# Decayed block attention and a squared-ReLU feed-forward: the attention's results are placed 64 bytes off the other operands within 256 bytes of on-chip memory

## The chip, the core and the metric

The kernel runs as one program on one core of a Trainium2 chip. The metric is the device time of one execution in microseconds. Of the kernel before there are three timed runs, 636.74, 637.0 and 637.23 us, with a median of 637.0 us. Besides, one execution was profiled; it took 637.8 us, of which 636.1 us lie between its first and its last instruction (the span).

## What is computed

```python
# attention with a decay, per batch b and head h; block of 64 positions, S = 768, D = 64, 4 batches, 8 heads
for each block:
    intra = (qb @ kb.T * Dmask) @ vb               # Dmask[i, j] = lam ** (i - j) for i >= j, else 0
    inter = (qb * lam_pow) @ kv_state
    out   = intra + inter
    kv_state = lam ** 64 * kv_state + (kb * rev_pow).T @ vb
# feed-forward on x = out, seen as 3072 tokens x 512 features
h = maximum(x @ w_in, 0)                           # w_in 512 x 2048
y = (h * h) @ w_out                                # w_out 2048 x 512
```

## The kernel before

**The tokens and the tiles.** The 3072 tokens are 24 chunks of 128 positions of one batch (`CHUNKS`), and three chunks make one tile of `N` = 384 tokens, so there are eight tiles (`TILES`). For each chunk two attention units (`q` = 0 and 1, four heads each) produce the attention's result, transposed, so that features lie on the 128 partitions and tokens along them. The first eight chunks run through `unit_plain` in float32, the other sixteen through `unit_split`, where every operand of a product is split into a high and a low float32r part.

**The tiles `xh` and `xl`.** The result of a unit is written to the tile `x` of its token tile, also as a high part (a copy on ScalarE, lines 382 and 497) and a low part (a subtraction on VectorE, lines 383 and 498). `x` has two buffers; each has an `xh` and an `xl` of 4 x 384 words a partition. These are the "attention's results" of the title.

**The feed-forward (`ffn`).** For each token tile and each of 16 blocks `f` of the 2048 hidden features, `mm1` (line 515) multiplies 12 times: for `(wih, xh)`, `(wih, xl)` and `(wil, xh)` four products each, one for each quarter `cc` of the 512 features. The stationary operand is a 128 x 128 piece of the weights, loaded into TensorE by a weight load (LDWEIGHTS) ahead of each product, and the moving operand is 384 words a partition of `xh` or `xl`. That is 8 x 16 x 12 = 1536 products. ReLU and square follow on ScalarE and VectorE (lines 529 to 536) and give `gh` and `gl`. The second products (`mm2`, lines 521, 522 and 524) take 128 x 128 pieces of `gh` or `gl` as the stationary operand and the 512 words of `woh` or `wol` as the moving one: 9 for each `f`, 1152 in all. From the third token tile on, the second products of two `f` run in one go after the first products of both.

**The order of the work.** `Plan` holds each operation with a guessed duration, a key and its buffers; `order` simulates the five engines and writes one fixed order for each of them. That order does not depend on addresses. The early part of the program (`early=True`: the preparation of the weights from 64-bit words, and `unit_plain`) uses its own buffers `pnt`, `diag0`, `diag1`, `st` and `m` (`EARLY`); when all of it has been issued, `late()` gives that memory back and makes the buffers of `unit_split` (`LATE`) in the same place. A late buffer waits for the last use of the early buffers that it overlaps. The packets `pkt` are the first of them to be filled, by DMAs on the SP queue (line 408).

**Where the buffers lie.** Tiles of a pool lie one after the other in the order of the calls that make them. Each takes a whole number of 256-byte units of a partition, but for two small tables that `unit_plain` and `unit_split` use as scales: `wdec` (8 words, 32 bytes) and `lc` (4 words, in a place of 32 bytes). They are the last of the permanent tiles (`const`). So in the kernel before every permanent tile (`gh`, `gl`, `g`, `hold`, `s1`, `vd`, `xh`, `xl`, `rdec`, all weights) starts 128 bytes past a multiple of 512; the early buffers behind the tables start 64 bytes further, at 192 past a multiple of 256 (`pnt0` at 190144); and `late()` puts a tile `space` of 112 words (448 bytes) ahead of the late buffers, which takes them to 128 past a multiple of 512 again (`pkt0` at 190592). `xh0` lies at 31872 and `wih0` at 59008.

Of the kernel before, what the change touches and what calls it, by code (L numbers as in the profile page):

```python
# [9 lines left out]
F32 = mybir.dt.float32  # L10
# [7 lines left out]
B, H, S, D = 4, 8, 768, 64  # L18
DM, DFF = 512, 2048
P = 128  # L20
C = 128
NC_ = S // C
NP = H // 2
# [130 lines left out]
LATE = ("pkt", "ab", "ka", "vv", "pp", "z", "zl", "ss0", "ss1")  # L154
# [13 lines left out]
def kernel(ctx: ExitStack, tc: tile.TileContext, pn, pk, lamx, w, out):  # L168
    nc = tc.nc
    const = ctx.enter_context(tc.tile_pool(name="const", bufs=1))  # L170
# [17 lines left out]
    def make(pool, kinds):  # L188
        for k in kinds:
            tiles[k] = [pool.tile(*shapes[k], name=f"{k}{'_' if k[-1].isdigit() else ''}{i}") for i in range(SLOTS[k])]  # L190

    make(ps, ("bank", "h"))
    make(const, [k for k in SLOTS if k not in EARLY + LATE + ("bank", "h", "x")])
    tiles["x"] = [[const.tile([P, NCC, N], F32R, name=f"{n}{i}") for n in ("xh", "xl")] for i in range(SLOTS["x"])]
    rdec = const.tile([P, NP, C], F32, name="rdec")

    flip, zero = tiles["g"][-1][:, 0:P], tiles["ob"][-1]
# [3 lines left out]
    wil = [const.tile([P, NCC, P], F32R, name=f"wil{f}") for f in range(NF)]  # L201
    woh = [const.tile([P, DM], F32R, name=f"woh{f}") for f in range(NF)]
    wol = [const.tile([P, DM], F32R, name=f"wol{f}") for f in range(NF)]

    wdec = const.tile([P, H], F32, name="wdec")
    lc = const.tile([P, NP], F32, name="lc")
    make(phase.enter_context(tc.tile_pool(name="early", bufs=1)), EARLY)

    def late():
        phase.close()  # L210
        pool = ctx.enter_context(tc.tile_pool(name="late", bufs=1, reuse_waits="tile"))
        pool.tile([P, 112], F32, name="space")
        make(pool, LATE)

        for k in ("ss0", "ss1"):
            for s in tiles[k]:
                nc.gpsimd.memset(s.bitcast(F32), 0.0)
# [395 lines left out]
    with tc.manual_schedule():  # L613
        for o in done:
            if o.early is False and not opened:
                assert n_early == 0, "an earlier buffer is still in use"
                late()
                opened = True
            o.fn()
            n_early -= o.early is True  # L620
# [43 lines left out]
```

## Time and profile before

| | |
|---|---|
| timed runs | 636.74, 637.0, 637.23 us; median 637.0 us |
| profiled execution | 637.8 us, span 636.1 us |
| TensorE clock granted over the span | 0.999 |
| first products (line 515) | 1536, each 128 x 128 stationary, 384 words moving |
| second products (lines 521, 522, 524) | 1152, each 128 x 128 stationary, 512 words moving |
| moved by DMA | 57.24 MB, a mean of 90 GB/s |

In the rows of the profile PE is TensorE's products, PEld its weight loads, DVE VectorE, ACT ScalarE, POOL GpSimd and SP the engine that issues the DMAs. [...] A row of the timeline that ends in x4 merges four products of one line; the distance between the starts of two such rows is the time of four.

### The profile page before, as it was taken

To read this page: it belongs to the slowest core of one execution; us is meant where nothing else is said; L and a number is where in the kernel's file an instruction comes from. 1 tells how busy PE (TensorE), PEld (TensorE's weight loads), DVE (VectorE), ACT (ScalarE), POOL (GpSimd) and SP (SyncE) were. 2 spreads that over 40 slices of the span, in tenths; PEclk is the share of its full clock that TensorE was granted. 3 is DMA by queue.
4 is the path that set the end of the run, shared out by engine and by line. 5 is a ranking of instruction groups with operands and counts; after the bars stand their busy time and mean duration, and the time that the engine had idled before them with its cause. 6 is when DMAs were issued, how large, how long until landed. Compare 5 with 4: busy or idle time off the path is not lost.

```text
span 636.1 us, 9584 instructions
## 1 busy us (share of the span) xinstructions
PE 627.1 (99%) x3608; PEld 570.4 (90%) x3608; DVE 476.6 (75%) x1078; ACT 360.9 (57%) x841; POOL 5.7 (1%) x15
## 2 busy tenths in 40 slices
PE   9899999999999999999999999999999999999997
PEld 7689999888999999999999999999999999999996
DVE  5999999946876998588965999659994799633222
ACT  5887777656755665366743766445753657522221
POOL 2000000000000000000000000000000000000000
PEclk9999999999999999999999999999999999999999
DMA  8825555513311220231203312121310411000001
GB/s 290 272 102 169 193 168 172 226 53 134 113 51 50 100 65 35 84 116 49 100 1 99 100 56 94 50 100 50 100 51 0 149 50 51 1 30 22 0 1 49
DMA packets 15166, 57.24 MB, mean 90 GB/s; under 512 B 1808, under 2 KB 1808, under 8 KB 15120
## 3 DMA queue, kind: packets, MB, share of 16 engines
q1 hardware_dynamic: 15120, 56.64, 26.2%
q8 instruction: 28, 0.46, 0.3%
q14 instruction: 18, 0.15, 0.1%
HBM read 50.34 MB, written 6.29 MB: 89 GB/s over the span
## 4 chain that ended last, share of the span: by engine, by line
PE 94%; DVE 3%; ACT 1%; DMA 1%; issue 0%
PE h L515 42%; PE bank L524 14%; PE bank L521 14%; PE bank L522 14%; PE bank L479 2%; PE bank L480 2%; PE bank L437 2%; PE bank L457 2%; PE bank L319 1%; PE bank L241 1%; PE bank L376 1%; DMA pkt<-pk 1%; DVE s L324 1%; DVE xr L379 0%; PE bank L373 0%; ACT diag L363 0%
## 5 line engine op out<-in xcount | busy, mean ns | idle before, releaser
L521 PE MATMUL bank<-woh,gh 128*128 128x512 f32 x384 | 150.8, 393 | 0.6 <-ACT gh L532 0.6
L522 PE MATMUL bank<-wol,gh 128*128 128x512 f32 x384 | 150.4, 392 | 0.0
L529 ACT ACTIVATE g<-h 128x384 f32<-128x384 f32 x128 | 62.9, 491 | 146.3 <-PE h L515 145.5
L515 PE MATMUL h<-xh,wih 128*128 128x384 f32 x512 | 112.5, 341 | 0.0
L515 PE MATMUL h<-xl,wih 128*128 128x384 f32 x512 | 109.9, 335 | 0.0
L515 PE MATMUL h<-xh,wil 128*128 128x384 f32 x512 | 109.3, 334 | 0.0
L535 DVE TENSOR_TENSOR g<-g 128x384 f32<-128x384 f32 x96 | 53.4, 556 | 69.0 <-ACT gh L534 68.9
L524 PE MATMUL bank<-woh,gl 128*128 128x512 f32 x384 | 100.7, 391 | 0.2 <-DVE gl L536 0.2
L515 PEld LDWEIGHTS h<-xh,wih 128*128 128x128 f32 x512 | 89.2, 188 | 5.3
L515 PEld LDWEIGHTS h<-xl,wih 128*128 128x128 f32 x512 | 91.8, 188 | 0.0
L515 PEld LDWEIGHTS h<-xh,wil 128*128 128x128 f32 x512 | 90.6, 188 | 0.0
L524 PEld LDWEIGHTS bank<-woh,gl 128*128 128x128 f32 x384 | 71.7, 188 | 15.1 <-DVE gl L536 0.3
L521 PEld LDWEIGHTS bank<-woh,gh 128*128 128x128 f32 x384 | 72.1, 188 | 14.4 <-ACT gh L532 0.8
L522 PEld LDWEIGHTS bank<-wol,gh 128*128 128x128 f32 x384 | 72.1, 188 | 13.3
L536 DVE TENSOR_TENSOR gl<-g,gh 128x384 fp32r<-128x384 f32 x128 | 70.8, 553 | 6.6 <-ACT gh L532 3.7
L534 ACT ACTIVATE gh<-g 128x384 fp32r<-128x384 f32 x96 | 50.5, 526 | 32.2 <-PE bank L522 30.9
L487 DVE TENSOR_TENSOR z<-bank,z 128x256 f32<-128x256 f32 x64 | 27.0, 421 | 25.9 <-ACT z L486 25.8
L448 ACT CAST pp<-s 128x512 fp32r<-128x512 f32 x32 | 19.9, 621 | 25.1 <-DVE s L446 25.1
L480 PE MATMUL bank<-pp,vv 128*128 128x256 f32 x128 | 31.8, 281 | 0.0
L479 PE MATMUL bank<-ab,ss 128*128 128x256 f32 x128 | 31.7, 281 | 0.0
L492 DVE TENSOR_TENSOR xr<-z,zl 64x256 f32<-64x256 f32 x64 | 26.7, 417 | 2.7 <-ACT zl L488 1.0
L570 DVE COPY ob<-bank 128x512 f32<-128x512 f32 x15 | 10.3, 689 | 22.1 <-PE bank L524 21.7
(80 smaller groups left out, 792.5 us busy)
## 6 DMA issues: line engine op xcount, KB each, us to landing
pkt<-pk SPq DMA_DIRECT2D x32, 768.0 KB, 4.3
st<-w SPq DMA_DIRECT2D x32, 512.0 KB, 3.4
pnt<-pn SPq DMA_DIRECT2D x16, 512.0 KB, 4.5
out<-ob SPq DMA_DIRECT2D x23, 256.0 KB, 2.3
out<-z SPq DMA_DIRECT2D x1, 256.0 KB, 2.0
g<-lamx SPq DMA_DIRECT2D x1, 6.0 KB, 1.7
```

Source lines behind the costliest of these rows:

```text
L479: nc.tensor.matmul(y4[:, n], at(ss)[:, n, h].rearrange("p t d -> p (t d)"), at(ab)[:, i], start=n == 0, stop=False, skip_group_check=True)
L480: nc.tensor.matmul(y4[:, n], at(vv)[:, i].rearrange("p t d -> p (t d)"), at(pp)[:, i], start=False, stop=True, skip_group_check=True)
L487: zo.append(add("DVE", 0.36, 2, lambda h=h, part=part: nc.vector.tensor_tensor(out=at(z)[:, h], in0=part(0), in1=at(z)[:, h], op=ALU.add), ...
L492: nc.vector.tensor_tensor(out=at(xr)[half(h)], in0=at(z)[0:64, h], in1=at(zl)[:, h], op=ALU.add)
L515: nc.tensor.matmul(at(h)[:, 0:N], wt[:, cc, :], xt[:, cc, :], start=k == 0, stop=k == 3 * NCC - 1)
L521: nc.tensor.matmul(at(os_[j]), at(gh)[:, sl], woh[f], start=f == 0, stop=False)
L522: nc.tensor.matmul(at(os_[j]), at(gh)[:, sl], wol[f], start=False, stop=False)
L524: nc.tensor.matmul(at(os_[j]), at(gl)[:, sl], woh[f], start=False, stop=f == NF - 1)
L529: orr = plan.op("ACT", 0.45, key, lambda: nc.scalar.activation(at(g), at(h)[:, 0:N], AF.Relu), [o1], [h, g])
L534: ogh = plan.op("ACT", 0.47, key, lambda: nc.scalar.activation(at(gh), at(g), AF.Square), [orr], [g, gh])
L535: og = plan.op("DVE", 0.48, key, lambda: nc.vector.tensor_tensor(out=at(g), in0=at(g), in1=at(g), op=ALU.mult), [orr, ogh], [g])
L536: ogl = plan.op("DVE", 0.48, key, lambda: nc.vector.tensor_tensor(out=at(gl), in0=at(g), in1=at(gh), op=ALU.subtract), [og, ogh], [g, gh, gl])
```

## The change

The two tables become two slices of one tile `tables` of 16 words (64 bytes), made ahead of `xh` and `xl`; a tile `space` of 48 words (192 bytes), which nothing uses, is made behind them; and the `space` of 112 words ahead of the late buffers goes.

```diff
     make(const, [k for k in SLOTS if k not in EARLY + LATE + ("bank", "h", "x")])
+
+    tables = const.tile([P, 16], F32, name="tables")
+    wdec, lc = tables[:, 0:H], tables[:, H:H + NP]
     tiles["x"] = [[const.tile([P, NCC, N], F32R, name=f"{n}{i}") for n in ("xh", "xl")] for i in range(SLOTS["x"])]
+    const.tile([P, 48], F32, name="space")
     rdec = const.tile([P, NP, C], F32, name="rdec")
...
     wol = [const.tile([P, DM], F32R, name=f"wol{f}") for f in range(NF)]
-
-    wdec = const.tile([P, H], F32, name="wdec")
-    lc = const.tile([P, NP], F32, name="lc")
     make(phase.enter_context(tc.tile_pool(name="early", bufs=1)), EARLY)

     def late():
         phase.close()
-        pool = ctx.enter_context(tc.tile_pool(name="late", bufs=1, reuse_waits="tile"))
-        pool.tile([P, 112], F32, name="space")
-        make(pool, LATE)
+        make(ctx.enter_context(tc.tile_pool(name="late", bufs=1, reuse_waits="tile")), LATE)
```

By the sizes, `xh` and `xl` start 64 bytes later (192 past a multiple of 256); `rdec`, `mask` and all weights start 256 bytes later, the early buffers 192 bytes later and the late buffers 256 bytes earlier, all at 128 past a multiple of 256. Within 256 bytes, `xh` and `xl` alone then lie off all the others, by 64 bytes. No instruction is added, removed or moved in its engine's order.

## The prediction

> **What bounds the kernel now.** I read the page first: the busy times, the chain that ended last, the costliest groups.
>
> ```profile
> span 636.1 us, 9584 instructions
> PE 627.1 (99%) x3608; PEld 570.4 (90%) x3608; DVE 476.6 (75%) x1078; ACT 360.9 (57%) x841; POOL 5.7 (1%) x15
> ...
> PE 94%; DVE 3%; ACT 1%; DMA 1%; issue 0%
> ...
> L521 PE MATMUL bank<-woh,gh 128*128 128x512 f32 x384 | 150.8, 393 | 0.6 <-ACT gh L532 0.6
> L522 PE MATMUL bank<-wol,gh 128*128 128x512 f32 x384 | 150.4, 392 | 0.0
> L529 ACT ACTIVATE g<-h 128x384 f32<-128x384 f32 x128 | 62.9, 491 | 146.3 <-PE h L515 145.5
> L515 PE MATMUL h<-xh,wih 128*128 128x384 f32 x512 | 112.5, 341 | 0.0
> L515 PE MATMUL h<-xl,wih 128*128 128x384 f32 x512 | 109.9, 335 | 0.0
> L515 PE MATMUL h<-xh,wil 128*128 128x384 f32 x512 | 109.3, 334 | 0.0
> ```
>
> TensorE has work for 627.1 of 636.1 us and makes 94% of the chain. ScalarE waits 145.5 us for the first products, not the other way round: line 521 sat idle 0.6 us for ScalarE, line 515 never. So time taken off or put on a TensorE product shows in the total, nearly whole. The change touches one thing that TensorE does 1536 times: it reads `xh` or `xl` as the moving operand while the weights of the next product are being loaded.
>
> What one product costs stands in the timeline of TensorE, late, where nothing else disturbs it:
>
> ```profile
> 568.62 1.52 PE L524 MATMUL bank<-woh,gl 128*128 128x512 f32 x6
> 569.98 0.87 PE L515 MATMUL h<-xh,wih 128*128 128x384 f32 x4
> 570.68 0.86 PE L515 MATMUL h<-xl,wih 128*128 128x384 f32 x4
> 571.39 0.85 PE L515 MATMUL h<-xh,wil 128*128 128x384 f32 x4
> 572.08 0.85 PE L515 MATMUL h<-xh,wih 128*128 128x384 f32 x4
> 572.77 0.85 PE L515 MATMUL h<-xl,wih 128*128 128x384 f32 x4
> 573.47 0.85 PE L515 MATMUL h<-xh,wil 128*128 128x384 f32 x4
> 574.16 0.39 PE L521 MATMUL bank<-woh,gh 128*128 128x512 f32 x1
> ```
>
> Starts are what counts. From 572.08 to 574.16 lie 12 first products, 173.3 ns each; from 568.62 to 569.98 six second products, 226.7 ns each. The 128 more columns cost 53.3 ns, so 384 columns cost 160.0 ns, and **13.3 ns a product are left that do not depend on its length**. They come with the change of weights, and they are not constant: the first four products behind line 524 take 0.70 us (175 ns each), the next four 0.71 us (177.5 ns), and only then does the pace settle. So the two streams into TensorE, moving operand and next weights, do something to each other, and it depends on how they stand in time. The question is whether it depends on the address too.
>
> **The change part by part.** The largest term first: does an offset of 64 bytes between the moving operand and the next weights cost or save anything? The kernel before holds a trial of it. While the last product of a group of line 515 streams, the weights of whatever comes next are loaded. In the first 160 us that is sometimes an early buffer (`pnt`, `diag`), which lies 64 bytes off `xh` within 256; later it never is. The recorded duration of a product shows whether it was stretched; these are the rows of line 515 by source for 0 to 160 us, and for 160 to 636 us:
>
> ```profile
> L515 PE MATMUL h<-xl,wih x112: 334/334/343, 25.5 to 158.4; 128*128 128x384 f32 x112
> L515 PE MATMUL h<-xh,wil x112: 334/334/339, 26.2 to 159.1; 128*128 128x384 f32 x112
> ...
> L515 PE MATMUL h<-xh,wil x400: 333/334/335, 161.1 to 623.8; 128*128 128x384 f32 x134
> ```
>
> A group ends with four products of `xh` and `wil`. After 160 us none of 400 exceeds 335 ns; before, the longest has 339. Three narrow windows show which ones: two where line 373, whose stationary operand is `diag`, follows (the windows 26.2 to 27.1 and 150.65 to 150.70), and one where line 457 follows, whose stationary operand is `pkt`, level with `xh` within 256 (158.0 to 159.6); their rows by source and from the timeline:
>
> ```profile
> L515 PE MATMUL h<-xh,wil x4: 334/334/338, 26.2 to 26.7; 128*128 128x384 f32 x4
> ...
> 26.22 0.86 PE L515 MATMUL h<-xh,wil 128*128 128x384 f32 x4
> 26.92 0.27 PE L373 MATMUL bank<-pnt,diag 128*128 128x128 f32 x1
> ...
> L515 PE MATMUL h<-xh,wil x3: 334/334/338, 150.3 to 150.7; 128*128 128x384 f32 x3
> ...
> L515 PE MATMUL h<-xh,wil x4: 334/334/334, 158.6 to 159.1; 128*128 128x384 f32 x4
> ...
> 158.56 0.85 PE L515 MATMUL h<-xh,wil 128*128 128x384 f32 x4
> 159.25 0.61 PE L457 MATMUL bank<-vd,pkt 128*128 128x128 f32 x4
> ```
>
> Both followers are float32 with 128 x 128 weights; they differ in where these lie. **With the next weights 64 bytes ahead of the moving operand the product takes 338 instead of 334 ns: 4 ns more.** So addresses matter within 256 bytes, and the size of what 64 bytes do is about 4 ns.
>
> The change makes the opposite offset: the moving operand 64 bytes ahead of the weights (192 against 128 past a multiple of 256). No row shows that one. Its bounds: at most all of the 13.3 ns is saved; at most 9 ns is lost, the longest product of the rows above (343 against 334), with the 4 ns of the trial and the 4.2 ns of the slow pace behind line 524 (177.5 against 173.3) well inside. Which value? The moving operand runs 384 words in 160.0 ns, 2.4 a nanosecond. The four products of line 457 above, each with a load of 128 words, take 0.61 us with a last one of about 0.27 (the row of line 373): (0.61 - 0.27) / 3 = 0.11 us from load to load, 1.1 words a nanosecond. So the moving stream is about twice as fast; it starts level with the weights and pulls ahead. If a clash happens wherever the two stand at the same place within 256 bytes, then level starts give a clash at the start, cut short because the streams already part, and one more each time that the moving stream has gained 256 bytes. Weights that lie 64 bytes ahead must be overtaken once in full: more, as seen. A moving operand that is already 64 bytes ahead leaves the clash at the start out: less. By size I take the same 4 ns, as a saving. This is an argument from one row and a guess at the mechanism, not a measurement.
>
> [...]
>
> What of the saving reaches the end depends on the stage:
>
> ```profile
> 30.00:95.00 65.00, 63.47 (x356) 57.35 (x357) 63.20 (x130) 48.42 (x99) 0.00 (x0) 1.00 0.48 163
> 95.00:160.00 65.00, 65.00 (x399) 57.38 (x398) 48.69 (x107) 42.08 (x93) 1.21 (x2) 1.00 0.41 146
> 160.00:540.00 380.00, 379.45 (x2105) 350.54 (x2104) 307.44 (x715) 221.84 (x529) 0.00 (x0) 1.00 0.22 71
> 540.00:636.00 96.00, 92.36 (x474) 83.77 (x472) 34.98 (x69) 27.49 (x57) 0.00 (x0) 0.99 0.05 17
> ```
>
> (Columns: stretch, its length, then busy time and count of PE, PEld, DVE, ACT, POOL; clock, DMA share, GB/s.) From 160 us on VectorE is busy 307.44 of 380 us, so a product sooner by 4 ns finds its partners ready: 3 x 400 = 1200 products x 4 ns = 4.8 us, all of it kept. From 30 to 95 us VectorE is busy 63.20 of 65 us; there the saving of the remaining 336 products, 1.3 us, would mostly turn into waits for VectorE. I keep half: 0.7 us. Sum: 5.5 us.
>
> **The smaller parts.** The second products, 1152 of them, keep their offset within 256 bytes (`gh` and `woh` both at 128); within 512 they become 256 apart. In the kernel before all permanent tiles are level within 512 too, so no row tells 256 from 512; I take nothing, and at worst 4 ns a product, 4.6 us, either way. The early products of lines 319, 347 and 373 become level with their partners; only the five or so stretched products above are concerned, 20 ns in all, which the offset of `xh` may return. The reads of the two tables move only in address: nothing. The late buffers overlap other early ones: by the sizes `pkt1` ended beside `pnt3` before (196736 to 202880 against 202432) and no longer does, so the second packet may be asked for sooner.
>
> ```profile
> 155.69 0.62 ACT L422 CAST ab<-pkt 128x512 fp32r<-128x512 f32 x1 [1.16 <-DMA pkt<-pk]
> ```
>
> ScalarE waits 1.16 us for that packet, but TensorE has other work and idles only the 0.6 us of line 521 quoted above; the gain is between nothing and 0.6 us, and I take nothing. No queue gets another order and no wait is added, so nothing new stands behind a waiting instruction.
>
> Against the profiled execution: 637.8 - 5.5 = 632.3 us. The median of the timed runs, 637.0, is 0.8 below that execution, so the forecast is **631.5 us**.
>
> **The rivals.**
>
> *The offset costs whichever sign it has.* For: the only offset that a trace shows costs, and of the paces that products show out of step (175 and 177.5 ns) both are slower than the level, settled one. Against: the two signs are not alike when one stream runs twice as fast. Place: line 515, each product; price 4 ns x 1536 = 6.1 us, none hidden because TensorE is the bound: 637.0 + 6.1 = **643.1 us**. It decides as soon as the settled pace is above 173.3 ns; at the longest product's 9 ns it would be 13.8 us and 650.8 us.
>
> *Nothing.* The pace settles by itself behind line 524, so the streams may find the same step again from any offset, the 13.3 ns being the price of the change of weights alone: 1536 x 0 ns, **637.0 us**. The trial shows only one product each time, not a settled run. [...] That the change would not do what it says is no rival of weight: the sizes give the addresses.
>
> *The whole 13.3 ns go.* 1200 x 13.3 = 16.0 us, and half of 336 x 13.3 = 2.2 us: 637.0 - 18.2 = **618.8 us**. Against: a level clash at the start is only a part of what is lost. [...]
>
> *The modulus is 512, not 256.* Then the second products change as well and the first ones lie 320 apart: anything between the cases, with 1152 more products at 4 ns: a spread of 4.6 us around them.
>
> **How the numbers follow.** About 0.2% (1.3 us) is what a measurement can tell from no change. Chances: the 4 ns saved 0.43 (its own range 627 to 635), the whole 13.3 ns 0.06, nothing 0.20, a cost near 4 ns 0.26, a larger cost 0.05. So faster 0.49, same 0.20, slower 0.31. The range reaches from 623 to 645.5: below lie the most of the fourth case, above the larger cost and some of the cost with the second products in it.
>
> **What would show it.** Right: the starts of line 515 lie 169 to 170 ns apart in a settled stretch, the recorded duration falls from 334 to about 330 ns, lines 521 to 524 stay at 226.7 ns, VectorE's share of the chain grows between 30 and 95 us. Wrong: 173.3 ns (nothing), 177 to 178 ns and 338 (the cost), or a changed pace of the second products (512). If the pace falls and the total does not, the waits of lines 521 and 524 for ScalarE and VectorE have taken it.

## The result and the profile after

The changed kernel takes 633.78 us (median of five runs, 633.21 to 634.31) where the kernel before takes 637.15 us in the same series (636.74 to 637.39). The ratio is 0.9949 with a 95% interval of 0.9937 to 0.9961, so 3.4 us less, between 2.5 and 4.0 us. The forecast was 631.5 us, 5.5 us less. The sign was right; more than a third of the size is missing, and the reason given for it turns out to be wrong.

The page after, busy times, chain and the groups that answer to those shown of before (the program's lines named here stand one higher than before):

```profile
span 631.5 us, 9583 instructions
PE 624.0 (99%) x3608; PEld 568.7 (90%) x3608; DVE 476.5 (75%) x1078; ACT 360.9 (57%) x841; POOL 5.9 (1%) x15
...
PE 96%; DVE 3%; ACT 1%; issue 0%
...
L520 PE MATMUL bank<-woh,gh 128*128 128x512 f32 x384 | 150.3, 392 | 0.0
L521 PE MATMUL bank<-wol,gh 128*128 128x512 f32 x384 | 150.1, 391 | 0.0
L528 ACT ACTIVATE g<-h 128x384 f32<-128x384 f32 x128 | 62.8, 491 | 144.2 <-PE h L514 143.4
L514 PE MATMUL h<-xh,wih 128*128 128x384 f32 x512 | 111.9, 340 | 0.0
L514 PE MATMUL h<-xh,wil 128*128 128x384 f32 x512 | 109.6, 336 | 0.0
L514 PE MATMUL h<-xl,wih 128*128 128x384 f32 x512 | 109.6, 336 | 0.0
```

TensorE still has work 99% of the span and makes 96% of the chain. The mean duration of a product of `xh` and `wil` has risen from 334 to 336 ns, in a kernel that became faster. In its trial, and in its signs, the forecast had read such durations as the time of a product. The starts say something else: in the rows below four products last 0.86 us and the next four start 0.69 or 0.70 us after them, so the durations overlap. Here is the timeline of TensorE at the place that was shown of before (there from 568.62 us on):

```profile
564.40 1.52 PE L523 MATMUL bank<-woh,gl 128*128 128x512 f32 x6
565.76 0.86 PE L514 MATMUL h<-xh,wih 128*128 128x384 f32 x4
566.46 0.85 PE L514 MATMUL h<-xl,wih 128*128 128x384 f32 x4
567.15 0.86 PE L514 MATMUL h<-xh,wil 128*128 128x384 f32 x4
567.85 0.86 PE L514 MATMUL h<-xh,wih 128*128 128x384 f32 x4
568.54 0.86 PE L514 MATMUL h<-xl,wih 128*128 128x384 f32 x4
569.23 0.86 PE L514 MATMUL h<-xh,wil 128*128 128x384 f32 x4
569.92 0.39 PE L520 MATMUL bank<-woh,gh 128*128 128x512 f32 x1
```

The last 12 first products, from 567.85 to 569.92, take 2.07 us (2.08 before): **the settled pace, the distance of starts once it no longer changes, is the same**. The first 12, from 565.76 to 567.85, take 2.09 us where they took 2.10 (569.98 to 572.08). The rows have steps of 10 ns, so the distances from start to start are needed; taken from the records of the trace and as medians over all places of a kind they are:

| products, behind what | before, ns | after, ns |
|---|---|---|
| first products behind the second ones of line 524 (57 places) | 171 175 178 185 176 182, then 173.3 | 177 176 173 169 170 176, then 173.3 |
| second products behind first ones (23 runs of 18) | 229 233 236 224 231 236 228 233 231, then 226.7 | 229 232 231, then 226.7 |
| second products behind the attention's line 437 (25 runs of 18) | 236 233, then 226.7 | 233 236 228 233 231, then 226.7 |

So in both kernels, whenever the length of the product changes, the next few products come at odd distances, and then the pace settles; the offset of 64 bytes changes only this start. (The operands change together with the length, so it is not told apart which of the two sets off the odd distances.) Behind a second product it saves 25 ns, behind a first product 28 ns; behind the attention it costs 11 ns.

Both programs issue the same products in the same order, so the two traces can be laid on each other product by product, and each difference of a distance put to its product. The spans differ by 4.58 us: 1.48 us are saved in the 1536 first products and 0.89 in the second ones, 0.18 are lost in the attention's, 0.71 are saved in one wait at 162 us, and 1.7 us in the first 35 us. That last part is put down to the single execution. More than half of it is one step into line 319, which starts at 31.3 us before: the step lasted 1.97 us before and 1.06 after, and between 0.15 and 2.18 us in the profiles below, whatever was changed. Ahead of it lie another 0.8 us, in the first 7 us; in all these profiles TensorE's 101st product starts somewhere between 12.7 and 13.7 us. Without it 2.9 us are left, inside the interval of the timed runs.

The wait is the one that the forecast bounded by 0.6 us and took as nothing. Before, and after, around the second products that follow the first `ab`, `ka`:

```profile
161.78 0.40 PE L437 MATMUL bank<-ab,ka 128*128 128x256 f32 x2
162.73 0.50 PE L521 MATMUL bank<-woh,gh 128*128 128x512 f32 x1 [0.55 <-ACT gh L532]
```

```profile
159.42 0.40 PE L436 MATMUL bank<-ab,ka 128*128 128x256 f32 x2
159.65 0.47 PE L520 MATMUL bank<-woh,gh 128*128 128x512 f32 x1
```

The idle time before the second products is gone. What removed it can be read from the waits of the SP queue, before and after: the request for the second packet waited 9.2 us for line 373, which reads the early `pnt` (by the sizes the packet's buffer overlapped the last of the four); with the late buffers 256 bytes earlier, 2.7 us. ScalarE's wait of 1.16 us for a packet, which the forecast showed, is not in the trace after.

```profile
SPq L408 <- PE bank L373: 9.2, 1, 9.2
```

```profile
SPq L407 <- PE bank L372: 2.7, 1, 2.7
```

### The profile page after: what moved, and what is told of

Read it like the earlier page. It is cut to its first block, busy times and chain, and to the rows that moved or that the text cites. A ratio compares the mean times of both kernels' runs of the same rounds, so it can differ in the third digit from the quotient of the medians.

```text
span 631.5 us, 9583 instructions
## 1 busy us (share of the span) xinstructions
PE 624.0 (99%) x3608; PEld 568.7 (90%) x3608; DVE 476.5 (75%) x1078; ACT 360.9 (57%) x841; POOL 5.9 (1%) x15
## 4 chain that ended last, share of the span: by engine, by line
PE 96%; DVE 3%; ACT 1%; issue 0%
PE h L514 42%; PE bank L523 14%; PE bank L520 14%; PE bank L521 14%; PE bank L479 2%; PE bank L478 2%; PE bank L436 2%; PE bank L456 2%; PE bank L318 1%; PE bank L240 1%; PE bank L375 1%; DVE s L323 1%; ACT diag L362 0%; PE bank L372 0%; DVE xr L378 0%; PE bank L346 0%
## 5 line engine op out<-in xcount | busy, mean ns | idle before, releaser
L514 PEld LDWEIGHTS h<-xl,wih 128*128 128x128 f32 x512 | 90.3, 188 | 0.0
```

What stands on the lines that cost most here:

```text
L514: nc.tensor.matmul(at(h)[:, 0:N], wt[:, cc, :], xt[:, cc, :], start=k == 0, stop=k == 3 * NCC - 1)
```

## The experiments

Two theories stood after the result. **A**: the offset acts through the products that have not settled after a change of length, and the move of the late buffers through one wait. **B**: the places of the early and late buffers make the gain, the offset little. Beside them stood the forecast's own mechanism, so many ns on every product. Line numbers differ by a few from kernel to kernel; the tiles' names tell the lines.

**The parts alone.** The offset without the rest, on the kernel before:

```diff
+    const.tile([P, 16], F32, name="ahead")
     tiles["x"] = [[const.tile([P, NCC, N], F32R, name=f"{n}{i}") for n in ("xh", "xl")] for i in range(SLOTS["x"])]
+    const.tile([P, 48], F32, name="behind")
```

> The kernel before with xh and xl 64 bytes later and everything behind them 256 bytes later; tables stay behind the weights, early buffers stay 64 bytes off, late buffers overlap the same early ones as before. Theory A (the offset acts only on products that have not settled after a change of length, the settled pace stays 173.3 ns): about 2.4 us below before, 12 first products behind line 524 take 2.08 us instead of 2.106, the 18 second products behind line 515 take 4.093 instead of 4.121; the wait of line 521 near 162 us stays. Theory B (the gain comes from where the early and late buffers lie): within 0.5 us of before.

Measured: 635.04 us against 636.68, ratio 0.9971 (0.9961 to 0.9981), 1.2 to 2.5 us less. The distances of the table are those of the changed kernel, within 1 ns, and worth 2.1 us in the trace. ScalarE again waits 1.2 us for a packet, and the wait of line 521 (here 523) stays in TensorE's timeline:

```profile
160.54 0.39 PE L439 MATMUL bank<-ab,ka 128*128 128x256 f32 x2
161.58 0.50 PE L523 MATMUL bank<-woh,gh 128*128 128x512 f32 x1 [0.65 <-ACT gh L534]
```

The rest without the offset, on the changed kernel:

```diff
     tables = const.tile([P, 16], F32, name="tables")
     wdec, lc = tables[:, 0:H], tables[:, H:H + NP]
+    const.tile([P, 48], F32, name="ahead")
     tiles["x"] = [[const.tile([P, NCC, N], F32R, name=f"{n}{i}") for n in ("xh", "xl")] for i in range(SLOTS["x"])]
-    const.tile([P, 48], F32, name="space")
```

> The changed kernel with all of the space ahead of xh and xl, so that they are level with every other operand within 256 bytes; early and late buffers as in the changed kernel. Theory A: 0.7 us below before (the wait near 162 us is gone), the settling as before, 2.106 and 4.121 us. Theory B: as the changed kernel, 3.4 us below before. If the period were 512 bytes, the second products, now 256 off gh, would change their pace or their settling.

Measured: 635.69 us, ratio 0.9986 (0.9977 to 0.9995), 0.3 to 1.5 us less. The distances of the table are those of the kernel before, and the wait is gone (0.72 us). Theory B falls with these two, and the parts add up within the intervals: 0.9971 and 0.9986 make 0.9957, against 0.9949 for both. This kernel also moves `woh` 256 bytes away from `gh`: the second products do not notice.

**Other offsets.** On the changed kernel, `xh` and `xl` 192 bytes off (for 128 bytes with 16 words ahead and 32 behind):

```diff
+    const.tile([P, 32], F32, name="ahead")
     tiles["x"] = [[const.tile([P, NCC, N], F32R, name=f"{n}{i}") for n in ("xh", "xl")] for i in range(SLOTS["x"])]
-    const.tile([P, 48], F32, name="space")
+    const.tile([P, 16], F32, name="space")
```

> The changed kernel with xh and xl 192 bytes ahead within 256, that is 64 bytes behind the weights, the offset that the trial in the trace before had. The prediction's own mechanism (4 ns on every product): settled pace 177 to 178 ns, 6 us above the kernel without an offset, near 642 us. Theory A: settled pace 173.3 ns again; only the settling differs, by at most 25 ns a change in either direction, so between 634 and 639 us. Theory B: as the changed kernel, 633.8 us.

> The changed kernel with xh and xl 128 bytes off within 256. Theory A: settled pace 173.3 ns, settling different again, between 634 and 639 us. The prediction's own mechanism: a settled pace other than 173.3 ns, between that of 64 and that of 192 bytes. Theory B: as the changed kernel, 633.8 us.

Measured: 192 bytes 638.13 us, ratio 1.0025 (1.0016 to 1.0034); 128 bytes 637.01 us, ratio 1.0006 (0.9997 to 1.0015). Here theory A falls in one point: it had the settled pace at 173.3 ns for every offset. The run with 192 bytes, at the same place of the program:

```profile
570.29 1.52 PE L524 MATMUL bank<-woh,gl 128*128 128x512 f32 x6
571.65 0.87 PE L515 MATMUL h<-xh,wih 128*128 128x384 f32 x4
572.35 0.87 PE L515 MATMUL h<-xl,wih 128*128 128x384 f32 x4
573.06 0.87 PE L515 MATMUL h<-xh,wil 128*128 128x384 f32 x4
573.77 0.87 PE L515 MATMUL h<-xh,wih 128*128 128x384 f32 x4
574.47 0.87 PE L515 MATMUL h<-xl,wih 128*128 128x384 f32 x4
575.18 0.87 PE L515 MATMUL h<-xh,wil 128*128 128x384 f32 x4
575.89 0.39 PE L521 MATMUL bank<-woh,gh 128*128 128x512 f32 x1
```

From 571.65 to 575.89 lie 24 products, 176.7 ns each, to the end of the group: they never come down to 173.3 ns. With 128 bytes it is 175.5 ns (24 products in 4.21 us), the distances 177, 174 and 175 ns in turn. Against the kernel without an offset, the first products of the 192 bytes cost 3.5 us and the second ones save 1.1, because behind such a group they start at 226.7 ns at once; the sum, 2.4 us, is the difference of the medians (638.13 - 635.69). For 128 bytes it is 1.9 - 0.8 = 1.1 us, measured 1.3. The recorded duration with 192 bytes is 338 ns (mean of the products of `xl`, and of `xh` and `wil`), the figure of the trial; with 128 bytes it is 338 too, at another pace.

These two kernels and the one without an offset differ in the place of `xh` and `xl` alone, and TensorE's settled pace is 176.7 and 175.5 ns against 173.3: at the same order of work the place alone is worth up to 3.4 ns a product here.

A smaller offset, 32 bytes:

```diff
+    const.tile([P, 8], F32, name="ahead")
+    tiles["x"] = [[const.tile([P, NCC, N], F32R, name=f"{n}{i}") for n in ("xh", "xl")] for i in range(SLOTS["x"])]
     tables = const.tile([P, 16], F32, name="tables")
     wdec, lc = tables[:, 0:H], tables[:, H:H + NP]
-    tiles["x"] = [[const.tile([P, NCC, N], F32R, name=f"{n}{i}") for n in ("xh", "xl")] for i in range(SLOTS["x"])]
-    const.tile([P, 48], F32, name="space")
+    const.tile([P, 40], F32, name="space")
```

> The changed kernel with xh and xl 32 bytes off instead of 64. If the settled 173.3 ns are a floor of the change of weights: 173.3 ns settled and only another settling, 633 to 636 us. If a smaller lead than 64 leaves part of a clash out: a settled pace below 173.3 ns, down to 169 (the shortest distances seen with 64), up to 6 us less.

Measured: 637.52 us, ratio 1.0008 (0.9999 to 1.0017); neither expectation. It has two settled paces in one program. The first fence is a group that follows a second product, the second one a group that follows line 480 of the attention; both are 24 first products with the same addresses within 256 bytes.

```profile
569.14 1.52 PE L524 MATMUL bank<-woh,gl 128*128 128x512 f32 x6
570.50 0.87 PE L515 MATMUL h<-xh,wih 128*128 128x384 f32 x4
...
574.74 0.39 PE L521 MATMUL bank<-woh,gh 128*128 128x512 f32 x1
```

```profile
322.08 0.28 PE L480 MATMUL bank<-pp,vv 128*128 128x256 f32 x1
322.20 0.86 PE L515 MATMUL h<-xh,wih 128*128 128x384 f32 x4
...
326.36 0.39 PE L521 MATMUL bank<-woh,gh 128*128 128x512 f32 x1
```

4.24 us against 4.16, 176.7 against 173.3 ns each. So the address alone does not fix the pace; with the same addresses the products of this kernel keep one of two rhythms. From 165 us on, every group behind a second product or behind line 457 keeps the slow one, and every group behind lines 437 and 480 the fast one: it goes with what ran before.

**Relative to what, and with what period?** The weights `wih` and `wil` moved by 64 bytes along with `xh` and `xl`:

```diff
     tiles["x"] = [[const.tile([P, NCC, N], F32R, name=f"{n}{i}") for n in ("xh", "xl")] for i in range(SLOTS["x"])]
+    wih = [const.tile([P, NCC, P], F32R, name=f"wih{f}") for f in range(NF)]
+    wil = [const.tile([P, NCC, P], F32R, name=f"wil{f}") for f in range(NF)]
     const.tile([P, 48], F32, name="space")
...
-    wih = [const.tile([P, NCC, P], F32R, name=f"wih{f}") for f in range(NF)]
-    wil = [const.tile([P, NCC, P], F32R, name=f"wil{f}") for f in range(NF)]
```

> The changed kernel with the weights wih and wil moved by 64 bytes together with xh and xl, so that moving operand and next weights are level again inside the first products, and both are off gh, woh and the attention's operands. Theory R (what counts is where the moving operand stands relative to the next weights, within 256 bytes): the settling inside the first products is that of no offset, 171, 175, 178, 185, 176, 182 ns behind the second products; settled pace 173.3. Rival Q (what counts is where the moving operand itself starts): as the changed kernel, 177, 176, 173, 169, 170, 176 ns.

Measured: 634.1 us, ratio 0.9951 (0.9936 to 0.9966). Behind second products the distances are 172 174 175 and then 173.3; behind line 457 they are 261 168 178 185 176 181 and then 173.3. Neither theory had named these sequences. Yet both are, but for their first distance, those of a kernel without an offset: 174 175 is what it does behind the attention, 178 185 176 182 what it does behind second products; and the 173 169 170 176 of the kernels with `xh` and `xl` alone 64 bytes ahead does not occur. A reading that fits, and that no run tests by itself: what a product does inside a group follows the offset to its own weights (Theory R); with which step a group begins follows the product before it, which runs while the group's first weights are loaded (in the kernel before, the last product of line 524 and the first load of line 515 both start at 569.75 us, the first product at 569.98), and this too now stood 64 bytes apart. Note what it means for the gain: here `xh` and `xl` are level with `wih` and `wil` again, and the time is still that of the changed kernel, within the intervals. The gain comes from how a group starts; a lead of the moving operand over its own weights is not needed for it. The rows of the timeline show a settled duration of 0.85 us for four, as before, and 0.86 with `xh` alone ahead:

```profile
568.55 0.85 PE L514 MATMUL h<-xh,wih 128*128 128x384 f32 x4
```

The period: 256 bytes more behind `xh` and `xl`, so that the weights come back to 128 past a multiple of 512:

```diff
-    const.tile([P, 48], F32, name="space")
+    const.tile([P, 112], F32, name="space")
...
-    nc = bacc.Bacc("TRN2", target_bir_lowering=False, num_devices=1, dynamic_dma_scratch_size=1024)
+    nc = bacc.Bacc("TRN2", target_bir_lowering=False, num_devices=1, dynamic_dma_scratch_size=512)
```

> The changed kernel with 256 bytes more behind xh and xl (and 512 less of scratch at the start of the memory, which nothing uses), so that all operands but xh and xl are level within 512 bytes, and xh and xl are 64 ahead within 512, not 320. If the period is 256: all distances and the time as the changed kernel. If it is 512: a different settling or pace of the first products, and the second products settle as in the kernel before.

Measured: 633.35 us, ratio 0.9940 (0.9924 to 0.9957), and every sequence of distances as in the changed kernel (the table above). For these tiles the period is 256 bytes: 512 is out by this run, and 128 or a part of it by the runs above, because 0 and 128 bytes (173.3 and 175.5 ns settled), and 64 and 192 (173.3 and 176.7), behave differently.

**More of the same.** `woh` and `wol`, the moving operands of the second products, also 64 bytes ahead:

```diff
+    woh = [const.tile([P, DM], F32R, name=f"woh{f}") for f in range(NF)]
+    wol = [const.tile([P, DM], F32R, name=f"wol{f}") for f in range(NF)]
     const.tile([P, 48], F32, name="space")
...
-    woh = [const.tile([P, DM], F32R, name=f"woh{f}") for f in range(NF)]
-    wol = [const.tile([P, DM], F32R, name=f"wol{f}") for f in range(NF)]
```

> The changed kernel with woh and wol, the moving operands of the second products, also 64 bytes ahead. Theory R: the second products behind line 436 (now 4.107 us for 18) and behind the first products (4.093) settle sooner or at once, 4.080 at the best, 25 x 0.027 + 23 x 0.013 = 1 us less; the settled pace stays 226.7 ns. But then the last second product, 64 off, meets the first weights of line 514, which changes the start of the first products in an unknown direction, by at most 25 ns x 57 = 1.4 us. 632.5 to 635 us.

Measured: 636.86 us, ratio 1.0001 (0.9992 to 1.0011): the whole gain is lost. The first products behave as well as in the changed kernel, but the second ones no longer settle at 226.7 ns. Behind the attention 19 of the 25 runs of 18 stay slow to their end:

```profile
205.51 0.40 PE L520 MATMUL bank<-woh,gh 128*128 128x512 f32 x1
205.75 0.40 PE L521 MATMUL bank<-wol,gh 128*128 128x512 f32 x1
...
208.08 0.40 PE L521 MATMUL bank<-wol,gh 128*128 128x512 f32 x1
208.32 1.56 PE L523 MATMUL bank<-woh,gl 128*128 128x512 f32 x6
209.72 0.34 PE L514 MATMUL h<-xh,wih 128*128 128x384 f32 x1
```

18 products from 205.51 to 209.72, by the records 4.203 us, 233.5 ns each with a settled 233.3; behind first products they run at 229 232 226 ns in turn, 229 in the mean. 64 bytes help the products of 384 words here and hurt those of 512. The second products lost 2.15 us where the offset of `xh` alone had won them 0.89.

**Does the gain go by changes or by products?** Both kernels with one block `f` at a time, first the one before, then the changed one:

```diff
-TWO, BOTH = 2, 9.0
+TWO, BOTH = 99, 9.0
```

> The kernel before with the second products run for one block f at a time all through (no pairs), so that the length of a product changes about twice as often. Theory A: each change costs extra time (first products 26 ns, second ones 28 to 41 ns before they settle), so this kernel is slower than before by about 60 more changes each way x 55 ns = 3 us, if no wait for ScalarE or VectorE comes on top: 640 us or more.

> The changed kernel with the same single blocks. Theory A (gain per change of length): against the single kernel without the offset it gains 0.7 us for the late buffers and about twice the 2.4 us of the paired one, 5 to 6 us in all. If the gain went with the number of products, which is the same: 3 us, as between the paired kernels.

Measured: 638.93 us (ratio to the kernel before 1.0038, 1.0024 to 1.0052) and 636.87 us (0.9997, 0.9988 to 1.0007), 2.1 us between them. The expectations were wrong, because their count was: the order is planned anew, puts the first products of two blocks together wherever it can, and leaves 39 groups of first products behind line 524, not twice 57. (The first products come in 74 groups instead of 102 and take 2.1 us less in the trace, the second ones in 112 instead of 76 and take 2.6 us more.) By the trace the first products gain 1.09 us here and 1.48 in the paired kernels, with 1536 products in each. By changes, with the same rates for both: 57 x 25 ns + 17 groups behind lines 437 and 480 x 5 ns - 20 behind line 457 x 2 ns = 1.47 us, and 39 x 25 ns + 26 behind line 437 x 5 ns = 1.10 us. By products both would be the same. The count of changes fits both.

**A better kernel?** The operands of the attention's products moved 64 bytes, behind the packets (192 in the second kernel, with 48 words in the gap):

```diff
-        make(ctx.enter_context(tc.tile_pool(name="late", bufs=1, reuse_waits="tile")), LATE)
+        pool = ctx.enter_context(tc.tile_pool(name="late", bufs=1, reuse_waits="tile"))
+        make(pool, LATE[:1])
+        pool.tile([P, 16], F32, name="gap")
+        make(pool, LATE[1:])
```

> The changed kernel with 64 bytes between the packets and the other late buffers, so that the operands of the attention's products (ab, ka, vv, pp, ss) lie level with xh and xl, 64 bytes off the weights and gh. Theory R: only the products next to a change between attention and feed-forward alter; the 25 runs of 18 second products behind line 436 (4.107 us each) go anywhere between 4.080 and 4.13, so 0.7 us less to 0.6 us more than the changed kernel: 633 to 634.5 us.

> The changed kernel with the same late buffers 192 bytes off instead of 64. Theory R: as the run with 64, the 25 runs behind line 436 between 4.080 and 4.13 us, 633 to 634.5 us; the products inside the attention are level with each other and keep their distances.

Measured: 634.07 us, ratio 0.9964 (0.9951 to 0.9977), and 633.51 us, ratio 0.9953 (0.9939 to 0.9968). The 25 runs behind line 436 take 4.105 and 4.111 us instead of 4.107. Neither differs from the changed kernel by more than the intervals, nor does the kernel whose other operands are level within 512 bytes (0.9940). What is left to gain in this way is small: the 25 and 23 runs of second products stand 27 and 13 ns above 18 x 226.7 = 4080 ns, together 1 us.

## Why the prediction came out as it did, by its steps

**What bounds the kernel** was right: TensorE was busy 99% before and after, and what its distances changed by shows in the total. The kernels with 192 and 128 bytes, 2.4 and 1.1 us by distances and 2.4 and 1.3 us by the timed runs, confirm it best.

**The trial was read rightly, though by a recorded duration; its extension failed.** Weights 64 bytes ahead of the moving operand (192 bytes off the other way) do cost, and not only once: 3.4 ns on each settled product, near the 4 ns of the forecast. The step that failed is "by size I take the same 4 ns, as a saving": a moving operand 64 bytes ahead saves nothing on a settled product, 173.3 ns with and without, which the forecast itself had named as a sign of being wrong. The argument from clashes while the streams part, a guess that no run shows as such, gave the sign of the one case that the trace had shown, and nothing for the other. The term 1200 x 4 ns + 0.7 us = 5.5 us became 1.5 us, made of some six products behind each change of length. The forecast had these unsettled products in view and used them as a bound only.

**The recorded duration** was a poor witness: settled products after the change are recorded with 336 instead of 334 ns at the same distance, where the forecast looked for 330, so a reading by durations alone would call the change a loss of 2 ns a product.

**The second products** were put at nothing, with 4.6 us either way if the period were 512. The period is 256 here (633.35 us with 256 bytes more behind `xh` and `xl`, 633.78 without), and they still gained 0.89 us: behind first products they settle after three products instead of nine. That this is because their first weights are loaded under the last product of `xh` (after, the load starts at 569.75 us, their first product at 569.92), which the offset moves, fits the distances but was not tested alone. **The packet** was put at nothing with a bound of 0.6 us; it gave 0.7. **Losses to VectorE** between 30 and 95 us, for which 0.6 us of the 1.3 were taken off, do not show: product by product the first products gain 0.23 us and the second ones 0.20 between 35 and 95 us, and no distance there grew by more than 0.04 us. Besides, only 173 of the 336 products that the sum put there lie in that stretch.

**The rivals.** "It costs whichever sign it has" is wrong for 64 bytes, but near the truth for the others tried: 32, 128 and 192 bytes all cost more than they save (ratios 1.0008, 1.0006 and 1.0025, against 0.9986 without an offset). "Nothing" was nearest in the settled pace, 173.3 ns at 64 bytes as without an offset, and wrong in taking the start for free (25 ns behind a second product); why the pace is the same is not shown. "All 13.3 ns go" and "the period is 512" are out: the 13.3 ns stayed with every offset tried, or grew. (They are worked out from two lengths, 384 and 512 words; no run has a third length, or products without a change of weights, so that they are one constant and come with that change is not shown.) The range, 623 to 645.5 us, came from these cases, and 633.78 lies well inside. That the forecast came within 2.3 us is in part luck: of the gain, 0.89 and 0.71 us came from two small terms that it had set to nothing.

Left open: why the place within 256 bytes counts at all, why 173.3 ns is kept at 0 and at 64 bytes, and why the same addresses can keep two rhythms (32 bytes, 173.3 and 176.7 ns). No run shows where in the chip the odd distances arise. 96 and 160 bytes were not run.

## What to carry to other kernels

Read products by the distance of their starts, never by their recorded durations (here 334 and 336 ns stood for the same 173.3), and separate the settled pace from the few products behind each change of shape. Where TensorE is the bound, the place of a moving operand within 256 bytes, against the other operands, was worth a few tenths of a per cent here, in either direction (0.9971 with 64 bytes alone; 638.13 against 635.69 us, 0.4%, with 192); it costs only a padding tile to try, but the 64 bytes that helped the products of 384 words here hurt those of 512 (636.86 us with both moved, 633.78 with the first alone). Moving buffers also changes which old ones they overlap (here one wait of the SP queue went from 9.2 to 2.7 us); look at that as a change of its own.

## What the runs showed that was not expected

- By the forecast's split, a settled product takes 160.0 + 13.3 ns at 384 words and 213.3 + 13.3 at 512, the same for offsets of 0 and 64 bytes in the first products; at 192 bytes and, behind second products, at 32 the rest is 16.7 ns.
- With 64 bytes the second products keep 233.3 ns behind the attention (19 runs of 25) and 229 behind first products: 20.0 and 15.7 ns above 213.3.
- The rhythm is exact: the six odd distances behind line 524 repeat within 1 ns at 53 of 57 places before and at 56 of 57 after, and again in the other kernels with the same offset. The four exceptions before lie at 38.6 to 124 us.
- In the first 35 us one and the same step lasted between 0.15 and 2.18 us in these profiles, a spread of more than half of the whole gain; a change of this size needs timed runs, or the comparison product by product.
